# Earlier loads, a split cast and new step times in an attention and token-mixing kernel on one core

**Chip, cores, metric.** One core of one Trainium2 chip. The metric is device time of one execution in microseconds (us). TensorE is called PE here, VectorE DVE, ScalarE ACT, GpSimd Pool and SyncE SP, as in the profile. A profile's span is about 1.7 us shorter than the run's time.

## The reference, cut to what matters

```python
# q, k, v: (8, 8, 576, 64); p: (8, 8, 32, 64)
def sm_attn(qq, kk, vv):
    s = scale * np.matmul(qq, kk.transpose(0, 1, 3, 2))
    a = np.exp(s - np.max(s, axis=-1, keepdims=True))
    return np.matmul(a / (a.sum(-1, keepdims=True) + 1e-09), vv)
p_packed = sm_attn(p, k, v)                 # 32 packed tokens per head
attn     = sm_attn(q, p_packed, p_packed)   # (8, 8, 576, 64)
# heads side by side: x is (8, 576, 512)
W_tok = scale * np.einsum('bsd,btd->bst', x @ w_q, x @ w_k)
out   = np.maximum(np.einsum('bst,btd->bsd', W_tok, x), 0) @ w_out
```

## The kernel before: the parts concerned

All work of a batch is cut into some twenty kinds of steps. Each has a time within the batch; step time plus batch times period is sorted, and the steps are issued in that order. The times only set each engine's order. Where the data of its next step are missing an engine stands, with the steps behind it: in the trace of the kernel before PE was idle for 1.85 us at `pr` until the cast of p was done.

```python
TIMES = ((16.10, {"lk": (-18.66,), "lv": (-6.60,), "lq": (-5.91,), "vc": (0.67,),
                  "kt": (0.00, 2.23, 0.41), "sa": (3.00, 5.24, 2.46), "pv": (6.73,),
                  ...                                          # cut
                  "pr": (2.76,)}),
         (16.09, {"mx": ..., "oa": ..., "ob": ...}))           # cut
todo = sorted((t + b * period, b, name, c)
              for period, times in TIMES for name, ts in times.items()
              for c, t in enumerate(ts) for b in range(B))
for _, b, name, c in todo:
    steps[name](b, c)
```

`lk`, `lv` and `lq` load k, q (cast to bf16 on the way) and v (float32) from Pool's queue. `vc` casts v. `kt` and `sa` transpose k and make the packed tokens' exponentials; `pv` multiplies these with v in 144 small matmuls, each with its own weight load. `qt`, `sc`, `sm`, `at` do the second attention, `pq`, `wk`, `wq`, `g`, `y`, `mx` the mixing, `oa` and `ob` the two halves of an output block.

```python
def pr(b, _):                      # batches 1, 3, 5: casts and transposes p of b+1 and b+2
    if b % 2 == 1 and b + 1 < B:
        p_transposes((b + 1) // 2)     # DVE cast of p_sb, 8 PE transposes, two copies

def sa(b, c):
    ...                                # cut: 24 matmuls, one exponential
    if b == 0 and len([n for n in st[0] if n[0] == "e1"]) == NC3:   # behind the third one
        for i, w in enumerate((moe_w_q, moe_w_k)):
            nc.scalar.dma_start(w_first[:, :, i * Dl:(i + 1) * Dl], ...)
        nc.scalar.dma_start(p_sb[:, 1:], p_v[:, 1:])

def vc(b, _):
    ...                                # cut: batch 0 comes in three pieces
    nc.gpsimd.tensor_copy(to[:, :, :, 0:Dh], v_in[b])

def pq(b, _):
    if b == 0:
        for i in range(2):             # i = 0 on ACT, i = 1 on DVE
            copy(i, wqk[:, :, i * Dl:(i + 1) * Dl], w_first[:, :, i * Dl:(i + 1) * Dl])
    ...
```

The softmax here doesn't subtract the row's maximum and nothing guards it: scores larger than these inputs give would overflow.

## Time and profile before

| | before |
|---|---|
| median time (3 runs) | 163.94 us |
| span of the profile, granted PE clock | 161.7 us, 0.926 |
| busy: PE, DVE, ACT, Pool | 77, 54, 49, 44% |
| start, up to `pv` of batch 1 | 37.3 us |
| six batches, `pv` of 1 to `pv` of 7 | 94.1 us |
| end | 30.3 us |

The prediction shows how these parts are read. The six batches in one line, from the view of stretches (start:end, length, busy time of PE, its weight loads, DVE, ACT and Pool, then granted PE clock, DMA share and GB/s):

```profile
37.27:131.40 94.13, 76.83 (x2102) 57.57 (x2120) 58.89 (x135) 50.89 (x117) 47.15 (x49) 0.96 0.78 202
```

In these traces the clock is 0.5 or 1 at any moment, so a mean of 0.96 means half clock for some 8% of the stretch. The cut at 131.40 lies 0.4 us ahead of the first matmul of that `pv`; cut at the matmul, the six batches take 94.5 us and the end 29.9.

### The profile page before, as it was taken

The numbers are of one execution on the slowest core, as the hardware profiler recorded it, in microseconds if no ns is written. First come the engines' busy times: TensorE is split into PE (matmuls) and PEld (weight loads), VectorE is DVE, ScalarE is ACT, GpSimd is POOL, SyncE is SP. The second block draws the span as 40 slices with busy tenths as digits, with TensorE's granted clock in tenths as the row PEclk, the third lists the DMA queues.
The fourth block names the chain that finished last, engine by engine and source line by source line (L and its number), as shares of the span: only waits on it lengthen the run. The fifth ranks groups of instructions, "written<-read, shape, count | busy, mean of one in ns | idle before, by whom it ended". The sixth has DMA issues, their size and how long they took to land.

```text
span 161.7 us, 6522 instructions
## 1 busy us (share of the span) xinstructions
PE 124.6 (77%) x2877; PEld 86.3 (53%) x2904; DVE 87.5 (54%) x197; ACT 79.1 (49%) x172; POOL 71.1 (44%) x84
## 2 busy tenths in 40 slices
PE   4588289469497995699935986999884989999950
PEld 1255166237375873477533863777464757755410
DVE  7642047623397788368720688467743875861300
ACT  3133004151176374557801574466832775878750
POOL 7960003673049654905960074907920690460000
PEclk9999759957999999999996898699999999999995
DMA  4999999008940599599989932499889440565584
GB/s 137 369 261 282 284 199 236 27 0 284 218 90 6 128 298 233 148 289 231 259 246 296 224 79 69 103 332 229 255 233 262 147 121 19 137 178 143 152 230 140
DMA packets 15532, 30.63 MB, mean 189 GB/s; under 512 B 2704, under 2 KB 5264, under 8 KB 15504
## 3 DMA queue, kind: packets, MB, share of 16 engines
q0 software_dynamic: 6512, 17.63, 46.2%
q1 hardware_dynamic: 7536, 11.93, 24.0%
q10 hardware_dynamic: 1456, 0.66, 1.9%
q8 instruction: 22, 0.36, 0.9%
q14 instruction: 6, 0.05, 0.1%
HBM read 30.15 MB, written 9.44 MB: 245 GB/s over the span
## 4 chain that ended last, share of the span: by engine, by line
PE 64%; DMA 11%; issue 10%; DVE 7%; ACT 5%; ACTq 1%; DVEq 0%
PE out_ps L415 16%; DMA p_sb<-in_p_dram 10%; PE T_ps L208 9%; PE pv_ps L255 7%; PE e_ps L303 5%; DVE p_nat L159 4%; PE warm_ps L192 4%; PE mix_ps L384 4%; PE e_ps L237 4%; PE aT_ps L324 4%; PE wk_ps L332 3%; PE wq_ps L343 2%; ACT o_sb L116 2%; PE g_ps L356 2%; DMA out_dram<-o_sb 1%
## 5 line engine op out<-in xcount | busy, mean ns | idle before, releaser
L415 PE MATMUL out_ps<-wout_w,relu 128*128 128x512 bf16 x109 | 33.3, 389 | 0.8 <-issue 0.8
L116 ACT ACTIVATE o_sb<-out_ps 128x512 f32<-128x512 f32 x36 | 21.2, 597 | 8.6 <-PE out_ps L415 6.4
L297 DVE COPY qT<-T_ps 128x768 bf16<-128x768 bf16 x24 | 13.4, 558 | 7.0 <-PE T_ps L208 5.8
L192 PE MATMUL warm_ps<-warm 128*128 128x512 bf16 x33 | 16.2, 536 | 1.2 <-DVE warm L172 1.2
L228 DVE COPY kT<-T_ps 128x768 bf16<-128x768 bf16 x24 | 12.7, 536 | 6.0 <-PE T_ps L208 5.7
L116 ACT ACTIVATE wk<-wk_ps 96x128 bf16<-96x128 f32 x16 | 4.3, 272 | 22.3 <-PE wk_ps L332 22.2
L303 PEld LDWEIGHTS <-qT 128*96 128x96 bf16 x192 | 11.9, 128 | 3.9 <-issue 2.5
L208 PE MATMUL T_ps<-ident,k_sb 128*128 128x128 bf16 x144 | 12.8, 231 | 1.3 <-DVE k_sb L114 0.7
L208 PEld LDWEIGHTS <-k_sb 128*128 128x128 bf16 x144 | 10.4, 104 | 5.7 <-issue 1.8
L208 PE MATMUL T_ps<-ident,q_sb 128*128 128x128 bf16 x144 | 13.0, 229 | 0.0
L326 DVE COPY aT<-aT_ps 128x384 bf16<-128x384 bf16 x24 | 8.4, 353 | 8.2 <-PE aT_ps L324 8.1
L415 PEld LDWEIGHTS <-relu 128*128 128x128 bf16 x128 | 10.6, 102 | 4.1 <-issue 0.4
L373 DVE TENSOR_SCALAR relu<-mix_ps 128x512 bf16<-128x512 f32 x16 | 10.5, 661 | 2.9 <-PE mix_ps L384 2.7
L259 DVE RECIPROCAL rec<-pv_ps 128x2 f32<-128x2 f32 x8 | 1.4, 171 | 19.5 <-PE pv_ps L255 19.5
L384 PE MATMUL mix_ps<-wqT,y 128*128 128x512 bf16 x31 | 11.0, 403 | 0.1
L208 PEld LDWEIGHTS <-q_sb 128*128 128x128 bf16 x144 | 9.8, 105 | 1.2 <-issue 1.0
L268 POOL TENSOR_TENSOR ppb<-pp,mask 128x256 bf16<-128x256 bf16 x16 | 10.4, 667 | 0.0
L375 ACT ACTIVATE relu<-mix_ps 128x512 bf16<-128x512 f32 x16 | 9.2, 611 | 0.5 <-PE mix_ps L384 0.5
L332 PEld LDWEIGHTS <-aT 128*96 128x96 bf16 x96 | 7.6, 131 | 3.4 <-issue 0.8
L237 PE MATMUL e_ps<-pT,kT 128*32 128x64 bf16 x576 | 8.5, 202 | 0.6 <-issue 0.5
L303 PE MATMUL e_ps<-ppT_106,qT 128*96 128x64 bf16 x96 | 6.7, 213 | 2.5 <-issue 2.4
L332 PE MATMUL wk_ps<-pqk,aT 128*96 128x64 bf16 x96 | 8.1, 210 | 0.6 <-issue 0.2
(311 smaller groups left out, 271.0 us busy)
## 6 DMA issues: line engine op xcount, KB each, us to landing
v_in<-in_v_dram POOLq DMA_DIRECT2D x7, 1152.0 KB, 6.6
q_sb<-in_q_dram POOLq DMA_DIRECT2D x8, 576.0 KB, 9.5
out_dram<-o_sb SPq DMA_DIRECT2D x24, 192.0 KB, 2.4
k_sb<-in_k_dram POOLq DMA_DIRECT2D x7, 576.0 KB, 12.2
out_dram<-o_sb SPq DMA_DIRECT2D x24, 128.0 KB, 2.8
out_dram<-o_sb SPq DMA_DIRECT2D x24, 64.0 KB, 2.6
k_first<-in_k_dram SPq DMA_DIRECT2D x3, 384.0 KB, 3.9
v_first<-in_v_dram SPq DMA_DIRECT2D x3, 384.0 KB, 6.2
```

The lines of the kernel that those rows point to most:

```text
L116: nc.scalar.activation(o, i, COPY)
L192: nc.tensor.matmul(ps, warm[:, 0:P], warm, start=True, stop=True)
L208: nc.tensor.transpose(ps[:, r, G, :], x_sb[:, G, sls[r]:sls[r] + 2, :].rearrange("a r d -> a (r d)"), ident)
L228: nc.vector.tensor_copy(kT, ps)
L237: nc.tensor.matmul(ps[m, r, G], kT[:, r, G, m], pT[:, b, G * NP + pos], start=True, stop=True)
L255: nc.tensor.matmul(ps[m, G, 0:Dh + 1], e1[m, r, G, par, :], v_sb[m, G, s, 0:Dh + 1], start=s == 0 and G == 0, stop=s == R - 1, skip_group_ ...
L297: nc.vector.tensor_copy(qT, ps.rearrange("a r G (pos s) -> a (G pos) r s", s=QP))
L303: nc.tensor.matmul(ps[:, :, h, :], qT[:, h].rearrange("a r s -> a (r s)"), st[b]["ppT"][:, h], start=True, stop=True)
L332: nc.tensor.matmul(ps[:, par, :], st[b]["aT"][:, G, c, par, :], st[b]["pqk"][:, G, Dl:], start=G == 0, stop=G == NG - 1)
L373: nc.vector.tensor_scalar_max(o, i, 0.0)
L384: nc.tensor.matmul(ps, yT[:, j * P:(j + 1) * P], wqT[:, 0:SM], start=True, stop=True)
L415: nc.tensor.matmul(ps, lhsT, wout_w[:, j, :], start=j == 0, stop=j == NJ - 1)
```

## The change

Its intent: loads early enough that none can be late, v's cast shared between Pool and DVE in thirds, and times from a new search with a shorter period.

```diff
-        (16.10, {
-            "lk": (-18.66,),
-            "lv": (-6.60,),
-            "lq": (-5.91,),
-            "vc": (0.67,),
-            "kt": (0.00, 2.23, 0.41),
-            "sa": (3.00, 5.24, 2.46),
-            "pv": (6.73,),
+        (13.00, {
+            "lk": (-21.58,),
+            "lv": (-17.17,),
+            "lq": (-16.52,),
+            "vc": (2.56, -0.25, 4.48),
+            "kt": (0.00, 1.08, 3.20),
+            "sa": (3.17, 4.37, 4.45),
+            "pv": (7.57,),
   (cut: the other steps' times)
-            "pr": (2.76,),
+            "pr": (-2.43,),
   (cut: mx, oa, ob)
-    dve_relu = (0, 1, 1, 0)
-    dve_wk = (0, 1, 0)
-    dve_out = (0, 0, 0, 0, 0)
-    dve_g, dve_y = 1, 0
+    dve_relu = (0, 0, 0, 1)
+    dve_wk = (1, 1, 0)
+    dve_out = (0, 0, 0, 0, 1)
+    dve_vc = (0, 0, 1)
+    dve_g, dve_y = 0, 0
-    def vc(b, _):
+    def vc(b, c):
+        sl = slice(c * KR, (c + 1) * KR)
+        o = v_bufs[b % NV][:, :, sl, 0:Dh]
         if b == 0:
   (cut)
+        elif dve_vc[c]:
+            nc.vector.tensor_copy(o, v_in[b][:, :, sl])
         else:
-            nc.gpsimd.tensor_copy(to[:, :, :, 0:Dh], v_in[b])
+            nc.gpsimd.tensor_copy(o, v_in[b][:, :, sl])
```

More of the change, by code (lines that the diff above doesn't have):

```diff
@@ L63 @@
     TIMES = (
-        (16.10, {
-            "lk": (-18.66,),
-            "lv": (-6.60,),
-            "lq": (-5.91,),
-            "vc": (0.67,),
-            "kt": (0.00, 2.23, 0.41),
-            "sa": (3.00, 5.24, 2.46),
-            "pv": (6.73,),
-            "pb": (19.95,),
-            "pt": (8.98,),
-            "pq": (21.08,),
-            "qt": (10.55, 13.14, 12.71),
-            "sc": (12.87, 15.04, 13.77),
-            "sm": (14.55, 19.55, 15.12),
-            "at": (22.27, 22.89, 21.67),
-            "wk": (24.66, 25.55, 23.04),
-            "wq": (29.65, 30.21),
-            "g": (28.60,),
-            "y": (30.56,),
-            "pr": (2.76,),
-        }),
-        (16.09, {
-            "mx": (38.10, 38.52, 36.27, 38.58, 45.80),
-            "oa": (56.28, 40.85, 48.55, 46.70, 50.18),
-            "ob": (57.42, 43.99, 52.01, 49.34, 52.86),
-        }),
-    )
-    dve_relu = (0, 1, 1, 0)
-    dve_wk = (0, 1, 0)
+        (13.00, {
[6 more added lines that the diff above has]
+            "pv": (7.57,),
+            "pb": (16.38,),
+            "pt": (8.90,),
+            "pq": (16.84,),
+            "qt": (9.51, 10.76, 7.84),
+            "sc": (10.92, 13.87, 10.45),
+            "sm": (12.13, 15.24, 11.86),
+            "at": (16.52, 18.39, 20.21),
+            "wk": (20.16, 21.01, 22.26),
+            "wq": (20.58, 25.73),
+            "g": (25.03,),
+            "y": (27.49,),
+            "pr": (-2.43,),
+        }),
+        (13.02, {
+            "mx": (30.92, 29.75, 29.33, 29.75, 31.56),
+            "oa": (44.18, 36.27, 40.19, 34.22, 40.47),
+            "ob": (45.18, 37.85, 41.19, 36.33, 41.68),
+        }),
+    )
+    dve_relu = (0, 0, 0, 1)
+    dve_wk = (1, 1, 0)
     dve_wq = (0, 0)
-    dve_out = (0, 0, 0, 0, 0)
-    dve_g, dve_y = 1, 0
+    dve_out = (0, 0, 0, 0, 1)
+    dve_vc = (0, 0, 1)
+    dve_a2 = (0, 0, 0)
+    dve_g, dve_y = 0, 0
     def pool(name, bufs, psum=False):
@@ L211, in transposes @@
         return ps
-    def vc(b, _):
-        to = v_bufs[b % NV]
+    def vc(b, c):
+        sl = slice(c * KR, (c + 1) * KR)
+        o = v_bufs[b % NV][:, :, sl, 0:Dh]
         if b == 0:
-            for c in range(NC3):
-                copy(c != 1, to[:, :, c * KR:(c + 1) * KR, 0:Dh], v_first[:, c])
+            copy(c != 1, o, v_first[:, c])
+        elif dve_vc[c]:
+            nc.vector.tensor_copy(o, v_in[b][:, :, sl])
         else:
-            nc.gpsimd.tensor_copy(to[:, :, :, 0:Dh], v_in[b])
+            nc.gpsimd.tensor_copy(o, v_in[b][:, :, sl])
     def kt(b, c):
@@ L314, in sm @@
         a2 = six.tile([CH, 2 * H, L], bf16, tag="a2", name="a2")
-        nc.gpsimd.tensor_tensor(a2, e2, rr.to_broadcast((CH, 2 * H, L)), op=MULT)
+        (nc.vector if dve_a2[c] else nc.gpsimd).tensor_tensor(
+            a2, e2, rr.to_broadcast((CH, 2 * H, L)), op=MULT)
         st[b]["a2", c] = a2.rearrange("a (x G pos) l -> a x G (pos l)", x=2, G=NG)
```

## The prediction

> **What bounds the kernel now.** I first read the page's busy shares: the TensorE (PE) is busy 77% of 161.7 us, no other engine above 54%, and the transfers of the three large queues fill 46.2, 24.0 and 1.9% of the 16 DMA engines. So no engine is full, and the next question is where PE stands idle. I cut the span at the start of each batch's `pv` (its probabilities times v) in the view of stretches; columns are start:end, length, then each engine's busy time, PE's granted clock, DMA share and GB/s.
>
> ```profile
> 0.00:37.27 37.27, 24.33 (x428) 14.72 (x433) 17.42 (x37) 10.04 (x17) 17.83 (x29) 0.84 0.79 197
> 50.98:65.72 14.74, 12.02 (x356) 9.08 (x358) 11.47 (x26) 8.32 (x21) 9.55 (x11) 1.00 0.79 199
> 80.44:102.20 21.76, 15.23 (x358) 10.75 (x360) 11.56 (x26) 9.67 (x22) 8.94 (x11) 0.87 0.68 176
> 102.20:116.10 13.90, 13.64 (x355) 9.98 (x357) 9.29 (x23) 9.09 (x21) 8.21 (x9) 0.95 0.95 248
> 131.40:161.70 30.30, 23.45 (x351) 13.99 (x352) 11.19 (x27) 18.14 (x39) 6.16 (x8) 0.94 0.50 140
> ```
>
> A good batch is PE-bound: 13.64 of 13.90 us busy. Six steady stretches, from `pv` of batch 1 to `pv` of batch 7, take 94.1 us; the start takes 37.3 and the end 30.3. What makes a batch slower is in the timeline of PE (start, length, instructions, idle before them and its cause):
>
> ```profile
> 62.64 0.41 PE L163 MATMUL pT_ps<-ident,p_nat 128*64 128x128 bf16 x8 [1.84 <-DVE p_nat L159]
> ...
> 68.28 0.38 PE L255 MATMUL pv_ps<-v_bf_85,e_1539 32*32 32x65 bf16 x25 [1.43 <-issue]
> ...
> 86.59 0.26 PE L324 MATMUL aT_ps<-perm,a_2071 96*128 96x96 bf16 x1 [3.54 <-issue]
> ```
>
> The idle called "issue" breaks groups in mid-row: 23 of 48 matmuls, idle, then 25. No data can be missing there. The page lists a queue of 22 packets that carries instructions:
>
> ```profile
> q8 instruction: 22, 0.36, 0.9%
> ```
>
> 0.36 MB in 22 packets is 16 KB a packet. I set the packets' times beside the count of PE instructions. Each long "issue" gap falls at a multiple of about 255 PE records (447, 1211, 1721, 2486, 2995, 3251, 4525, 4780, 5290), and the gap ends 1.2 to 1.5 us after such a packet lands. The packet for the next block starts 0.5 to 1 us after PE enters the present one when no load is in flight, but 2.4 to 7.5 us after when a burst of loads is. A block that PE uses up faster than that ends in a stall, and `pv` alone is 288 instructions in 1.2 us. Such stalls after 37 us sum to 12.0 us (2.08, 0.62, 1.43, 0.72, 3.54, 0.94, 2.15, 0.56). Missing loads cost nothing there: no steady-state wait is put down to k, q or v.
>
> The start hangs on one transfer, as the chain that ended last shows (start, length, what):
>
> ```profile
> 16.53 13.54 DMA p_sb<-in_p_dram
> 30.09 1.14 DVE p_nat L159
> ```
>
> [...] while k and wout were loading, the queue of w_first and p_sb got about one packet for each of theirs (178 against 142 in the 2 us after 24 us). [...] the trace has half-clock stretches of 3.4 and 6.8 us, after idle at 16 to 20, 29 to 34, 83 to 87 and 96 to 98 us.
>
> **The change, part by part.** The step times only set each engine's order, so I sorted them for both kernels. PE's work is the same: 5,800 instructions.
>
> *Loads.* On Pool they stay where they were, three in a row behind `pb`; what differs is the batch. Before, behind pb of batch b came v and q of b+1 and k of b+2; now all three are of b+3. As no wait for them was on the path, being earlier saves nothing by itself. Two effects remain. The last burst falls near `pv` of batch 5, not of 6, so one burst fewer can delay instruction blocks. And v and q of batch 2 join the queue in the first 12 us.
>
> *The start.* That last effect meets the transfer of p. It is issued at 16.53 as before (behind the first three exponentials) and must pass 256 more packets of v and 256 of q. At one packet for one, with packets of 218 and 194 ns beside its own 46 ns (records of those queues), these take (218+46)x256/16 = 4.2 and (194+46)x256/16 = 3.8 us. p had some 560 packets left when k of batch 2 was through, at about 26.5, so it lands at about 34.7, not 29.7. At the same time step `pr`, which needs it, moves ahead: from behind kt of batch 1 (2.76+16.10 = 18.86) to 10.57, ahead of the last q transposes of batch 0, two of its three scores, and all of kt and sa of batch 1. VectorE and PE run in order, so both stop there from about 24.5 to 35.5, and PE then starts at half clock. What is left before `pv` of batch 1 is 6.7 us at full clock (24.69 to 29.4 and 31.27 to 37.27 in the trace, less waits), so 9 to 11 with the slow clock: `pv` of batch 1 begins near 46, not 37.3. **Plus 8.7 us.**
>
> *Casts of v.* Pool loses 2.10 us per batch and gains two thirds of that, 1.40; VectorE gains one 128x768 cast, 0.55 (the same shape from k_first takes 0.546). Pool is 44% busy and VectorE 54%: off the path. With relu, wk, g and output copies reassigned, ScalarE takes about 0.3 us more per batch (one relu of 0.61, g's 0.29 and less of wk's and an output), VectorE nearly none. Three relus now follow each other on ScalarE with pqk and three exponentials ahead of `pv`, 4.1 us of work where PE has 3.3: a small wait, 1 us in all six batches.
>
> *Order of PE.* Counting instructions through the new order tells where the blocks of 255 end. Short blocks, by the durations of the groups: 1.9 us (batch 1), 1.8 (2), 2.6 (3), 1.15 (4), 1.25 (5), 3.0 (6), 2.7 (7). Against about 3 us of undisturbed refill, and 5 or more within a burst (which will begin near the end of `pv`), that makes about 1, 1.7, 1, 1.9, 2.5, 0.3, 0.3: 8.7 us, of which 8.4 before `pv` of batch 7, against 11.5 there now. **Minus 3.1.** The later casts of p find only one third of a v cast on Pool beside them, and stand behind a score group in PE's order: waits of about 1.0 each, not 1.84. **Minus 1.7.** With the 3.5 us hole gone its half-clock stretches go too: **minus 3.**
>
> *Sum.* Start 46.0. Steady: 94.1 - 3.1 - 1.7 - 3 + 1 for ScalarE + 1.3 for output work done earlier = 88.6. End: 30.3 - 1.3 for that work - 0.3 for the stall + 0.8 because three of the last four relus share ScalarE = 29.5. That is 164.1 in the profile's span, against 161.7: plus 1.5%, or 166.4 us of the median of 163.94. I take off 2.4 because the order came from a search and I priced its stalls from few cases: **164.0 us**.
>
> **Rivals.** (1) *The start stays as it was and the steady gains are bare.* It would hold if p's packets passed faster, or if work held up at the start were hidden later. For it: PE after `pr` has a compact backlog, and before, too, it did little between 16 and 37 us. Then 161.7 - 8 + 1 = 155 in span, about 157 us. (2) *Refill stalls grow.* The bursts now start with k, its packets 2,304 B, and come a little earlier in the batch; if block fetches inside `pv` wait 5 to 7 us as at 66.7 and 82.8, add 5: 169 us. (3) *ScalarE or VectorE becomes the bound.* Estimated busy 10.6 and 10.8 us in a batch of 13 to 14.5: against it. If it came, about 0.5 us per batch: 167. (4) *The loads are hidden anyway* and only noise is left: 164; it agrees with my number by another way.
>
> **Range and chances.** The three runs before spread from 161.62 to 165.97, 2.7%. The start is uncertain by 2.5 us, stalls by 3, the rest by 2; together 4.4, so about 6 us either way: 157.5 to 170. Faster by over 2% needs under 160.7: 0.29. Slower by over 2%, above 167.2: 0.24. Within: 0.47.
>
> **What would show it.** Right: the cast of p of batches 2 and 3 starts at 34 to 36 us, with 8 us or more of idle PE before it and `pv` of batch 1 after 43; the steady six batches take 86 to 91 us; "issue" gaps at multiples of 255 records, summing to 7 to 10 us; no wait for k, q or v. Wrong: p landing by 30 (then packets do not alternate as I count), or steady batches under 13.5 us, which would make the change clearly faster; or new waits of PE on ScalarE of over 0.5 us a batch.

## The result

The changed kernel takes **173.74 us** (median of 4, 173.0 to 175.63) against 163.07 (median of 4): the ratio of the fast runs is 1.067, 95% interval 1.053 to 1.082. It is clearly slower, outside the predicted range. The ratio is the mean time of one kernel's fast runs over that of the other's of the same rounds, so not quite the ratio of the medians quoted.

Here a run counts as slow when it is over 1.5% above its kernel's fastest. On this one core times spread without a gap, 158.9 to 169.0 for the kernel before in 55 runs. For many kernels too few runs are left as fast, so I give medians of all runs too, and say where the two disagree. The profile of the changed kernel is of a run of 175.63, slow by this rule, 1.5% above the fastest; a second one (e1, 173.57, also slow) has the same parts.

| part | before | predicted | after | e1, the same kernel |
|---|---|---|---|---|
| start | 37.3 | 46.0 | 49.8 | 50.2 |
| six batches | 94.5 | 88.6 | 95.0 | 92.7 |
| end | 29.9 | 29.5 | 29.1 | 28.8 |

The same parts in the view of stretches of the changed kernel:

```profile
0.00:49.79 49.79, 25.38 (x438) 15.58 (x442) 19.66 (x40) 10.05 (x17) 19.72 (x32) 0.77 0.74 186
49.79:144.77 94.98, 79.53 (x2118) 59.33 (x2138) 60.12 (x138) 54.02 (x124) 45.29 (x54) 0.92 0.71 183
144.77:173.90 29.13, 21.98 (x333) 12.95 (x336) 9.95 (x24) 16.56 (x36) 4.46 (x6) 0.94 0.50 137
```

In the start PE is busy as long as before, 25.4 us against 24.3, within 12.5 us more. The steady part has not become shorter, and its clock is lower, 0.92.

PE's timeline tells where it stood (start, length, instructions, idle before them and what ended it):

```profile
11.35 0.51 PE L210 MATMUL T_ps<-ident,k_sb 128*128 128x128 bf16 x6 [1.60 <-ACT k_sb L118]
...
36.21 0.64 PE L165 MATMUL pT_ps<-ident,p_nat 128*64 128x128 bf16 x8 [11.36 <-DVE p_nat L161]
...
45.82 0.29 PE L293 MATMUL pqk_ps<-wqk,ppT_106 64*32 64x128 bf16 x8 [2.93 <-DVE wqk L116]
...
56.47 0.51 PE L210 MATMUL T_ps<-ident,q_sb 128*128 128x128 bf16 x6 [3.34 <-issue]
...
101.91 0.40 PE L259 MATMUL pv_ps<-v_bf_86,e_2154 32*32 32x65 bf16 x14 [5.54 <-issue]
```

The second gap is the step `pr` waiting for p, the great loss of the start. Before, PE waited at the same step for 1.85 us:

```profile
31.27 0.41 PE L163 MATMUL pT_ps<-ident,p_nat 128*64 128x128 bf16 x8 [1.85 <-DVE p_nat L159]
```

The transfer of p in the changed kernel is in the chain that ended last (start, length, what), and the DMA issues give size and time to landing:

```profile
17.60 18.24 DMA p_sb<-in_p_dram
```

```profile
p_sb<-in_p_dram ACTq DMA_DIRECT2D x1, 384.0 KB, 18.2
```

p now takes 18.2 us instead of 13.5 to land and is awaited ahead of all of `kt` and `sa` of batch 1. The 5.54 us at 101.91 breaks a group of 48 matmuls: a refill of instructions, as the prediction reads such gaps. A packet of the queue `q8 instruction` runs from 99.61 to 100.58 us and PE goes on 1.33 us after it has landed, while a burst of loads is in flight (its packets run from 95.1 to 106.6 us). e1 has the same gap of 5.54 us at the same place.

### The profile page after: what moved, and what is told of

The parts are those of the page before. It is cut to its first block, busy times and chain, and to the rows that moved or that the text cites.

```text
span 173.9 us, 6543 instructions
## 1 busy us (share of the span) xinstructions
PE 126.9 (73%) x2879; PEld 87.9 (51%) x2904; DVE 89.7 (52%) x200; ACT 80.6 (46%) x176; POOL 69.5 (40%) x91
## 4 chain that ended last, share of the span: by engine, by line
PE 60%; DMA 14%; issue 10%; DVE 4%; ACT 3%; POOL 3%; SPq 1%; ACTq 1%
PE out_ps L420 15%; DMA p_sb<-in_p_dram 10%; PE T_ps L210 10%; PE pv_ps L259 6%; PE e_ps L307 5%; PE mix_ps L389 4%; DMA v_first<-in_v_dram 4%; PE warm_ps L194 3%; PE e_ps L241 3%; PE aT_ps L329 3%; PE wq_ps L348 3%; PE wk_ps L337 2%; PE g_ps L361 2%; DVE wqk L116 1%; PE ppT_ps L278 1%
## 5 line engine op out<-in xcount | busy, mean ns | idle before, releaser
L118 ACT ACTIVATE o_sb<-out_ps 128x512 f32<-128x512 f32 x32 | 18.8, 594 | 7.0 <-PE out_ps L420 5.6
L301 DVE COPY qT<-T_ps 128x768 bf16<-128x768 bf16 x24 | 13.4, 558 | 12.6 <-PE T_ps L210 12.5
L194 PE MATMUL warm_ps<-warm 128*128 128x512 bf16 x34 | 17.2, 549 | 1.2 <-DVE warm L174 1.2
L354 ACT ACTIVATE wqT<-wq_ps 128x288 bf16<-128x288 f32 x16 | 6.6, 414 | 22.7 <-PE wq_ps L348 22.7
L210 PE MATMUL T_ps<-ident,q_sb 128*128 128x128 bf16 x144 | 13.7, 238 | 3.5 <-issue 3.3
L232 DVE COPY kT<-T_ps 128x768 bf16<-128x768 bf16 x24 | 12.5, 532 | 7.0 <-PE T_ps L210 6.7
L210 PE MATMUL T_ps<-ident,k_sb 128*128 128x128 bf16 x144 | 13.6, 235 | 2.9 <-ACT k_sb L118 1.6
L420 PEld LDWEIGHTS <-relu 128*128 128x128 bf16 x128 | 11.1, 103 | 6.0 <-issue 0.9
L380 ACT ACTIVATE relu<-mix_ps 128x512 bf16<-128x512 f32 x24 | 13.7, 606 | 0.4
L210 PEld LDWEIGHTS <-q_sb 128*128 128x128 bf16 x144 | 10.6, 109 | 5.1 <-issue 4.4
L272 POOL TENSOR_TENSOR ppb<-pp,mask 128x256 bf16<-128x256 bf16 x16 | 12.6, 806 | 0.0
L165 PE MATMUL pT_ps<-ident,p_nat 128*64 128x128 bf16 x32 | 2.1, 270 | 14.1 <-DVE p_nat L161 14.1
L319 POOL TENSOR_TENSOR a_534<-e_490,rr 96x512 bf16<-96x512 f32 x1 | 1.0, 1039 | 27.4 <-DVE rr L317 27.4
L389 PE MATMUL mix_ps<-wqT,y 128*128 128x512 bf16 x32 | 10.4, 382 | 0.3 <-ACT y L118 0.3
L118 ACT ACTIVATE pT<-pT_ps 64x512 bf16<-64x512 bf16 x4 | 2.4, 592 | 17.1 <-DVE pT L116 17.1
## 6 DMA issues: line engine op xcount, KB each, us to landing
v_in<-in_v_dram POOLq DMA_DIRECT2D x7, 1152.0 KB, 10.2
```

The lines of the kernel that those rows point to most:

```text
L118: nc.scalar.activation(o, i, COPY)
L194: nc.tensor.matmul(ps, warm[:, 0:P], warm, start=True, stop=True)
L210: nc.tensor.transpose(ps[:, r, G, :], x_sb[:, G, sls[r]:sls[r] + 2, :].rearrange("a r d -> a (r d)"), ident)
L232: nc.vector.tensor_copy(kT, ps)
L272: nc.gpsimd.tensor_tensor(ppb[:, G], st[b]["pp"][:, G, 0:1, :].to_broadcast((P, NP, Dh)), mask, op=MULT)
L301: nc.vector.tensor_copy(qT, ps.rearrange("a r G (pos s) -> a (G pos) r s", s=QP))
```

## The experiments

Sixteen runs were made, of eleven new kernels; the others repeat one of these or the change. "Mean" is the ratio of the means of all runs, "fast" that of the fast runs (a dash where one alone was fast). The runs e1 to e4 share a chip, so do e5 to e8, e9 to e12 and e13 to e16. "Steady" is `pv` of batch 1 to `pv` of batch 7 in the run's profile, "issue" PE's idle time so named within it, summed from the timeline (0.15 us and more). Weighed by fast runs alone, at 2%, the record calls the change slower, and every experiment "unclear" or, with too few fast runs, nothing at all; so what the profiles show is firmer below than what the times show.

| run | median us (runs) | before | mean | fast | `pv` of 1 at | steady | issue |
|---|---|---|---|---|---|---|---|
| before | 163.07 (4) | | | | 37.3 | 94.5 | 12.7 |
| after | 173.74 (4) | 163.07 | | 1.067 | 49.8 | 95.0 | 14.1 |
| e1 the change again | 174.66 (4) | 162.66 | 1.058 | - | 50.2 | 92.7 | 13.8 |
| e2 the change, `pr` late | 160.10 (4) | 162.66 | 0.977 | - | 38.9 | 92.9 | 8.5 |
| e3 the change, old load lead | 170.71 (4) | 162.66 | 1.042 | 1.037 | 44.9 | 92.1 | 12.8 |
| e4 before, `pr` early | 164.59 (4) | 162.66 | 1.005 | 1.004 | 41.0 | 89.0 | 10.2 |
| e5 before, `pr` late | 161.38 (4) | 164.01 | 0.976 | - | 35.6 | 90.8 | 6.8 |
| e6 e2, no loads from batch 3 | 151.40 (4) | 164.01 | 0.920 | 0.923 | 39.8 | 82.4 | 2.7 |
| e7 e2, v cast whole | 166.00 (4) | 164.01 | 1.007 | 1.013 | 37.4 | 96.4 | 9.1 |
| e8 e2, loads a batch later | 163.95 (4) | 164.01 | 0.996 | 0.994 | 38.1 | 94.2 | 4.6 |
| e9 e2, `pv` in thirds | 160.28 (20) | 164.08 | 0.976 | 0.982 | 35.3 | 93.3 | 5.5 |
| e10 e9, weights cast on ACT | 158.86 (4) | 164.08 | 0.964 | - | 34.1 | 93.9 | 7.4 |
| e11 e10, v from SP's queue | 160.30 (20) | 164.08 | 0.977 | 0.981 | 36.8 | 90.5 | 5.2 |
| e12 e2 again | 161.26 (20) | 164.08 | 0.985 | 0.995 | 37.0 | 93.6 | 9.0 |
| e13 e10, weights loaded first | 156.66 (6) | 164.87 | 0.951 | 0.944 | 32.3 | 94.7 | 5.5 |
| e14 e10 again | 156.47 (6) | 164.87 | 0.952 | 0.956 | 33.2 | 91.3 | 6.6 |
| e15 e7 again | 165.66 (22) | 164.87 | 1.006 | 0.983 | 39.9 | 97.3 | 11.2 |
| e16 e2 again | 162.40 (6) | 164.87 | 0.989 | 0.986 | 37.8 | 93.7 | 9.0 |

All but e6 give the right result. In e9 to e11, e13 and e14 the first third of `pv` stands earlier in the order, so their `pv` of 1 at is not to be compared with the others' to within 1 or 2 us.

**The start: where `pr` stands.** Theory A: the change lost its time to `pr`, at which DVE and PE stop until p has landed. Rival: the start only waits elsewhere. e1 is the changed kernel as it is, to be the measure on this chip.

> The changed kernel itself once more, for a profile in the fast state and a ratio of the same rounds. All theories: ratio to before 1.06 to 1.08; cast of p of batches 2 and 3 starts near 35 us after 10 to 12 us of idle PE; idle called issue of 12 to 16 us after the start.

It did as expected by its median (174.66 to 162.66); one of its four runs, the only fast one, took 168.01, which is 1.036 of the fast runs of before. So the size of the loss is known to some 3% only.

e2 moves one step and nothing else:

```diff
-            "pr": (-2.43,),
+            "pr": (8.00,),
```

> The changed kernel with one step moved: the cast and transposes of p for the batches after next go from 10.57 to 21.0 (behind pv of batch 1 in every engine's order; first needed by batch 2). Theory A (PE and VectorE stand still at this step until p lands, and nothing makes up for it): the 11 us of idle PE shrink to a wait for the weights' transfer of 0 to 4 us, pv of batch 1 begins at 39 to 42 us, time falls by 8 to 11 us to 162 to 166. Rival B (the time is lost in steady batches or to refills of instructions, the start only waits elsewhere): time falls by under 4 us.

14.6 us less by the medians, more than expected; 10.4 us less between the one fast run of each (157.65 and 168.01), as expected. By mean and median it is faster than the kernel before. PE's timeline of e2:

```profile
33.84 0.40 PE L293 MATMUL pqk_ps<-wqk,ppT 64*32 64x128 bf16 x8 [2.90 <-DVE wqk L116]
42.14 0.41 PE L165 MATMUL pT_ps<-ident,p_nat 128*64 128x128 bf16 x8 [0.85 <-DVE p_nat L161]
```

The 11.36 us at `pr` have become 0.85, while p landed no sooner (its last packet starts at 36.2 us in the trace, 36.0 in e1). The next wait in line, 2.90 us for the weights, is as long as in the change. `pv` of batch 1 begins 11.3 us earlier than in e1. Theory A holds, and the step's place alone makes up more than the whole loss.

e4 asks the same from the other side, with the kernel before:

```diff
-            "pr": (2.76,),
+            "pr": (-3.01,),
```

> The kernel before with one step moved, the other way: the cast of p for the later batches at the place that the change gives it (from 18.86 to 13.09 of 16.1 a batch). Theory A: VectorE and PE stop at it from about 24 to 30, pv of batch 1 moves from 37.3 to 42 to 45, time plus 4 to 7 us: 167 to 171. Rival: the work behind it is hidden by the later waits, within 2 us of before.

```profile
30.96 0.64 PE L163 MATMUL pT_ps<-ident,p_nat 128*64 128x128 bf16 x8 [7.93 <-DVE p_nat L159]
```

The wait is there, 7.93 us, and `pv` of batch 1 comes 3.7 us later than in the profile before, at 41.0 instead of 42 to 45. It moves by less than the wait because the waits before of 1.85 us for p and 1.92 us for the weights are taken up in it (0.81 us is left at the weights). But the time rose only by 1.9 us in the median, 0.4% in the fast runs: a miss for theory A, and the rival's number ("within 2 us of before") came true. Its profiled run had a steady part of 89.0 us, 5.5 us less than before, so the profile can't exclude that some of the start was made up later. With steady parts of one kernel varying by 2 us between profiles (95.0 and 92.7 for the change), 3.7 us of start are hard to see in four runs; the reverse test leaves theory A open for the kernel before.

e5 moves `pr` of the kernel before the other way, to 10.60.

> The kernel before with the cast of p for the later batches moved later too (from 18.86 to 26.7 of 16.1 a batch, behind the second batch's pv). Theory A: its own waits of PE for p and for the cast at 29 to 33 us go, pv of batch 1 begins 1 to 3 us earlier than 37.3, time 159 to 162; then the step times of the change, freed of this step, are worth little more than this. Rival: the wait is taken over whole by the cast of the weights behind it; no change within 1 us.

161.38 against 164.01, ratio of the means 0.976 (its one fast run: 158.19), and `pv` of batch 1 begins at 35.6, 1.7 us earlier, as theory A had it. The kernel before with this one step moved is as fast as the changed kernel with it moved (0.977, 0.985 and 0.989 in e2, e12 and e16). So all else in the change, new order, splits and earlier loads together, is worth nothing that these runs can show.

**The start: loads ahead of p.** e3 gives the changed kernel's loads the lead that they had before, counted in batches:

```diff
-            "lk": (-21.58,),
-            "lv": (-17.17,),
-            "lq": (-16.52,),
+            "lk": (-15.07,),
+            "lv": (-5.33,),
+            "lq": (-4.77,),
```

> The changed kernel with the loads at the same lead in batches as before (k 1.16, v 0.41, q 0.37 of a batch ahead). Theory: p no longer queues behind v and q of batch 2, lands near 30 instead of 35.8, so 4 to 6 us less: 167 to 170. Rival (the lead of the loads is not what delays p): p lands at 34 to 36 and the time stays at 172 to 175.

```profile
31.34 0.64 PE L165 MATMUL pT_ps<-ident,p_nat 128*64 128x128 bf16 x8 [4.91 <-DVE p_nat L161]
```

p's last packet starts at 30.6 us instead of 36.0, the wait is 4.91 us instead of 11.1 in e1, and `pv` of batch 1 begins 5.3 us earlier: v and q of batch 2 in the queue delay p by about the 5 us that the prediction gave them. The median falls by 4.0 us, at the edge of what was expected; but the two fast runs of e3 (167.86 and 168.33) are no faster than the one of e1 (168.01), so a gain in the whole time is not shown.

Are the early loads needed? e8 takes e2 and shifts all three by one batch (each time plus 13).

> e2 with all loads one batch later (k, v and q of batch b+2 behind pb of batch b, and only batch 1's at the start). Theory (the weights and p queue behind the loads of batch 2): the weights land by 26 and p by 28 us, the wait of 2.9 us for the weights' cast goes, time 2 to 4 us under e2: 156 to 158. Rival (loads needed this early): waits for k, v or q of over 1 us a batch and more time than e2.

The last packet of p starts at 27.0, as the theory said. But the wait for the weights stayed at 2.90, and new waits came:

```profile
107.67 0.51 PE L210 MATMUL T_ps<-ident,k_sb 128*128 128x128 bf16 x6 [1.00 <-DMA k_sb<-in_k_dram]
124.61 0.82 PE L210 MATMUL T_ps<-ident,k_sb 128*128 128x128 bf16 x6 [3.46 <-DMA k_sb<-in_k_dram]
```

The rival was right: with 8.58 of 13 us as its lead k is late, and e8 is no faster than before. The lead of 1.16 batches that k had before is enough: in e3, with that lead, no wait for k, q or v is listed behind those of batch 0. The change's longer lead (half a batch for k, nine tenths for v and q) delays p at the start, and has no return that shows.

Why the 2.90 us did not go, though the weights had landed at 26.6, shows in the timelines of DVE and Pool in e8, beside that of DVE in the kernel before:

```profile
30.38 2.50 DVE L116 CAST wqk<-w_first 64x512 bf16<-64x512 f32 x1
31.94 1.94 POOL L272 TENSOR_TENSOR ppb<-pp,mask 128x256 bf16<-128x256 bf16 x2
```

```profile
33.01 0.35 DVE L114 CAST wqk<-w_first 64x512 bf16<-64x512 f32 x1
```

The same cast took 0.35 us while Pool was all but idle (its next instruction starts at 33.23), and 2.50 us beside Pool's casts and products from 27.37 to 33.84 us. Its end follows Pool, and not its own start: it came 0.28 us after the first of the two `ppb` products ended (32.60), and so it did in nine other profiles (the change, e1 to e3, e6, e7, e12, e15, e16), by 0.28 to 0.29 us, though the cast had begun 1.06 to 3.03 us earlier. So in these runs the "wait for the weights" was a wait for Pool's chain, and an earlier transfer could not shorten it.

**The steady part: refills of instructions.** Theory C: they wait behind the bursts of loads. Rival D: they are slow by themselves, or the stores delay them. e6 is e2 with a wrong result: no loads from batch 3 on.

```diff
     def load_k(b):
+        if b > 2:
+            k_in[b] = k_in[2]
+            return
   (cut: the same for q and v)
```

> e2 without any load of k, q, v from batch 3 on (wrong result on purpose: batches 3 to 7 use batch 2's inputs). Theory C (blocks of instructions wait behind the bursts of loads): after the start the issue gaps of PE sum to 3 to 6 us, not 8 to 14, none over 2 us from batch 2's pv on, the six steady batches take 82 to 87 us, not 93, and the run 148 to 154. Rival D (refills are slow by themselves, or the stores delay them): gaps stay at 8 us or more and the time falls by under 3 us.

The steady part of e6, then that of e16, which is e2 with its loads:

```profile
39.80:122.20 82.40, 76.86 (x2139) 56.34 (x2142) 59.97 (x140) 54.45 (x125) 36.87 (x42) 0.99 0.27 71
```

```profile
37.80:131.50 93.70, 80.66 (x2135) 58.25 (x2134) 60.14 (x140) 54.45 (x125) 45.38 (x54) 0.94 0.71 184
```

The same work takes 11.3 us less. The issue gaps fall from 9.0 to 2.7 us, all other idle from 4.0 to 2.8, and the clock rises from 0.94 to 0.99: half clock for 10.6 us, against 1.4, which costs up to 4.6 (an estimate: half of the difference). Theory C holds, with gaps even under the 3 to 6 us expected, in so far as the loads as a whole are the cause: without them, the rest of the work at this order runs at 13.7 us a batch. e6 also frees Pool of issuing them (54 instructions against 42), but PE's idle time for other causes than issue fell by 1.2 us only. The clock, too, fell behind the long stalls: in e16 half clock follows the gaps of 2.36 and 3.53 us, and none follows those of 0.83 to 1.30. The stores have a part too: ahead of the 3.54 us hole of the kernel before, the refill's packet started 1.8 us after its block was entered, while stores filled 71% of the DMA engines and loads 20% (packets that start from 81.5 to 83.25 us), and then took 2.00 us beside the loads, about double the 0.98 us that is the median of the 22 such packets of that trace.

e9 attacks the stall from the other end: `pv` in three steps of 96 instructions with other work between.

```diff
-            "pv": (7.57,),
+            "pv": (5.30, 6.30, 7.57),
   (cut: oa of block 3 from 34.22 to 33.25, its ob from 36.33 to 34.30)
-    def pv(b, _):
+    def pv(b, c):
+        if c == 0:
+            st[b]["pv"] = psum(w_pool, [P, NG, VW], fp32, "pv_ps")
+        ps = st[b]["pv"]
-        for s in range(R):
+        for s in range(c * KR, (c + 1) * KR):
   (cut: the rest of `pv` runs with the third step alone)
```

> e2 with pv in three steps of 96 instructions each, the first and second with an output half, a transposition and a mix between them, the third behind an earlier output half; no instruction is added. Theory C [...]: blocks around pv last longer, the issue gaps after the start sum to 4 to 8 us instead of 9 to 14, time 2 to 5 us under e2's 160. Rival: gaps only move to other places, within 1 us of e2.

Beside e12, the same chip and 20 runs each: 160.28 against 161.26, 0.982 against 0.995 by the fast runs. The issue gaps fell from 9.0 to 5.5 us, into the expected band; the time fell by 1 to 1.5 us, less than expected. The intervals of the two ratios overlap (0.976 to 0.989; 0.984 to 1.006), so the gain is likely, not shown. A new wait of 0.69 us for v stands ahead of the earlier `pv` of batch 2.

> e2 once more, as the measure of the other runs of this call on the same chip: 0.97 to 1.00 of before.

e11 breaks up the burst: v of batches 4 to 7 is issued by SP between two stores.

> e10 with v of batches 4 to 7 loaded from the SyncE queue between two stores, some 3 us of PE's order after k and q, so that a burst is k and q alone. Theory C: shorter bursts beside pv, refill delays there fall from 4 us, 1 to 3 us less. Rival: the bytes are the same and the delays only spread: no change within 1 us, or waits for v.

160.3 against 158.86 of e10 and 160.28 of e9: the rival. In its profile the issue gaps are shorter than in e10 (5.2 against 7.4 us) and so is the steady part, while the start is 2.7 us longer; in 20 runs nothing is gained.

**Casts of v.** e7 is e2 with v cast whole on Pool.

> e2 with v cast whole on Pool again, in one instruction. Theory (off the path): within 1.5 us of e2's 160. Rival (the split saves a wait ahead of pv): 2 us or more slower, with waits of PE for the v cast in pv.

166.00 against 160.10 of e2: the rival's number, but on another chip, so it was run again beside e2:

> e7 (v cast whole on Pool) beside e2 on one chip, since they were on different chips. If the split of v's cast itself saves time: 2 to 5 us slower than e16. If e7 was slow by its chip: within 1.5 us of e16.

> e2 for the third time, as the measure of e15 on the same chip: 0.97 to 1.00 of before.

PE's timeline of e15:

```profile
34.83 0.40 PE L290 MATMUL pqk_ps<-wqk,ppT 64*32 64x128 bf16 x8 [3.95 <-DVE wqk L116]
...
56.55 1.51 PE L256 MATMUL pv_ps<-v_bf,e 32*32 32x65 bf16 x144 [1.17 <-POOL v_bf L220]
```

Both gaps are of the same length in e7's profile: at the weights' cast 1.05 us longer than in e2 and e16, where Pool's casts of v are short, and a wait of 1.17 for v in batch 2. Those 2.2 us are shown, and so is that the rival had the wait right. By the medians e15 is 3.3 us slower than e16, and by the means 2.7, but the fast runs of both are equal (0.983 and 0.986), so how much of it stays in the whole run is not settled.

**A better version.** e10 adds to e9 that both halves of the weights' cast run on ACT (`copy(0, ...)` for `copy(i, ...)`).

> e9 with both halves of the weights' cast on ScalarE. Theory (the cast on VectorE took 1.06 to 2.50 us beside Pool's work and held PE 2.9 us at pqk): wait at pqk of batch 0 shrinks by 0.5 to 1.5 us and pv of batch 1 begins that much earlier; the whole run changes by as little.

> e10 once more with more rounds, as the measure of e13: 0.96 to 0.98 of before.

e14 took 156.47 us against 164.87 of before, fast ratio 0.956 (0.943 to 0.970). The wait for the weights was 3.43 us in e10's profile, 1.57 in e14's; and on ACT the second half of the cast starts as soon as the weights land (31.07 and 30.79). What of the gain over e9 is this cast, I cannot tell from so few runs.

e13 also issues the weights' loads first of all on ACT's queue, and casts them behind the third exponential.

> e10 with the two loads of the weights issued first of all on ScalarE's queue (before: behind the third exponential, in the middle of the loads) and cast there behind the third exponential. Theory: PE's wait of 3.4 us at pqk of batch 0 goes, and p has fewer packets ahead of it; the first k pieces land up to 1 us later; pv of batch 1 begins 2 us earlier than in e10; time 1 to 3 us under e10. Rival: a new wait in the start takes its place, within 1 us of e10.

The wait at `pqk` is gone from the timeline and p's last packet starts at 25.6, but 156.66 us is e14's time: the first `kt` pieces waited 2.15 us instead of 1.42 for k, and the steady part of its profile was 3.4 us longer. The rival, within the spread of these runs. Both versions take about 5% less than the kernel before, and by the ratios to it some 10% less than the change.

## Why the prediction was wrong

Its direction of the start and the way that p is delayed were right. Three terms of its sum were mis-sized, and a fourth had no ground. The sum of 164.1 us came out 173.9 in the profile: 3.8 us of the difference lie in the start, 6.4 in the six batches and -0.4 in the end. Its own rival (2), "Refill stalls grow", because the bursts "come a little earlier in the batch", is what came in the steady part.

1. **"Order of PE ... Minus 3.1."** The refill stalls of the steady part were to be 8.4 us, against 11.5 before; counted in the same way, without gaps under 0.5 us, they were 13.7 (with the small gaps 14.1, against 12.7). The step that failed is the cost of a refill in batches 1 and 4: it was priced near "about 3 us of undisturbed refill", because the burst "will begin near the end of `pv`". There PE took 6.2 and 6.8 us from entering one block to going on in the next (2.9 and 3.05 in the estimate), and the stalls were 3.34 us (estimated 1) and 5.54 (estimated 1.9). In the other four batches the stalls sum to 4.8 us, against 5.5 estimated, each within 1 us. I had counted Pool's chain behind `sc` as longer than PE's path to the end of `pv`. In fact the first load of the burst was issued 3.2 us ahead of the start of `pv` in batch 1 and 1.2 ahead in batch 4, and 1.4, 0.3 and 0.3 us behind it in batches 2, 3 and 5; its packets follow 1.5 to 1.8 us later. That the earlier burst is the whole cause of these two stalls is not shown: in batch 4 of the kernel before 4.3 us of stalls came with a burst issued 0.7 us behind the start of `pv`, and in e16 batch 4 had 1.0 us with a burst issued 0.6 ahead. No run moves the burst alone. Pool's and PE's lines of batch 4:

```profile
93.58 0.77 POOL L128 DMA_DIRECT2D k_sb<-in_k_dram  x1
```

```profile
94.81 0.88 PE L259 MATMUL pv_ps<-v_bf_86,e_2058 32*32 32x65 bf16 x48
```

   Moreover, my range of refill delays ("2.4 to 7.5 us") was read too widely: where a block's first instruction had itself waited, I counted from the block before it. Counted from the end of the stall, a refill started 2.4 to 4.6 us after PE entered the block within a burst, in the kernel before.

2. **"With the 3.5 us hole gone its half-clock stretches go too: minus 3."** The hole did not go, it became 5.5 us. Half clock in the steady part rose from 8.2 us to 14.8 (10.5 in e1): up to 3.3 us more (half of the rise, an estimate) instead of 3 less. Of the two half-clock stretches meant, of 3.4 us each, one stands behind the hole, but the other, from 100.1 us, behind a wait of 1.84 us for the cast of p. What sets it is not shown: behind the same wait of 1.84 us at 62.64, and behind the gap of 2.15 at 124.5, the same trace has none.

3. **"Plus 8.7 us"** for the start was 12.5. The cast of p began at 35.86, inside the predicted 34 to 36, and PE was idle 11.36 us. Two waits were left out: 1.60 us (4.05 in e1) at the second piece of k, whose cast on ACT stands behind one of v that waits for its load (before, that piece came last), and 2.93 us at `pq` for the weights' cast on DVE, 2.28 us long, again until 0.28 us after Pool's product. I had taken the trace "less waits", and such a wait stood there before too, 1.92 us.

4. **"I take off 2.4"** because the order came from a search. The sum without it was 166.4; the search's order earned nothing (e5 beside e2).

Right were: no wait for k, q or v behind those of batch 0 in the changed kernel; issue gaps at block ends; waits of PE on ACT in the steady part under 0.3 us; the end, 29.1 against 29.5. Better than predicted were the later casts of p: no wait of 0.2 us or more, not 1.0 each, at 0.29 us a cast. That the end came so near is not evidence for its three terms, which no run tests singly. "Off the path" for v's cast was off by some 2 us early on (e7, e15), and VectorE's third of the cast, put at 0.55 us, took 0.75 to 1.82 us in batches 2 to 7, beside Pool's work.

Some readings of the working were wrong without moving its sum. Behind `pb` of batch b, the kernel before issues v and q of b+2 and k of b+3, not of b+1 and b+2. The gaps are multiples of 255 PE records apart, but do not stand at such multiples (447 is the first). In the 2 us after 24 us, k and wout together have 174 packets against the 178 quoted; 142 are k's alone.

## What to carry to other kernels

Here one early step that waited for a late transfer held up all the work behind it on its engine (11.36 us of idle PE at `pr`, 0.85 with the step moved, e2): before moving a step, ask when its data land, and when its result is first needed (here 1.4 batches later). Loads further ahead than their first use required were not free: with them in the queue p, which the start hangs on, took 18.2 us to land, and 11.8 in e3 without. And where PE stalls in mid-group without a data wait, look at the queue that carries instructions and count instructions per microsecond (in the kernel before PE went on 1.2 to 1.5 us after such a packet had landed, at stalls that are multiples of 255 PE records apart); whether it pays to spread the dense groups is not settled here (e9: likely, 1 to 1.5 us). Last, the wait put down to DVE's cast of the weights was here a wait for Pool (the cast ended 0.28 to 0.29 us after a Pool product in ten profiles): compare when a wait ends over several runs, not only how long it is.

## What the traces show of refills, casts and queues

- Refills of instructions, for a PE with some 2,900 matmuls and as many weight loads: 12.7 us of issue gaps in 94.5 us before, 14.1 of 95.0 after, and 2.7 of 82.4 without loads (e6). In the kernel before, counted in blocks of 255 PE records, the packet for the next block starts 0.5 to 1.1 us after PE enters a block with no load in flight and 2.4 to 4.6 us after it within a burst; the 22 packets take 0.9 to 2.0 us each; and at a stall PE goes on 1.2 to 1.5 us after the packet has landed.
- Casts of DVE beside Pool's work: the 64x512 cast from float32 took 0.35 us with Pool all but idle (the kernel before), 1.06 (e2), 2.28 (the change) and 2.50 us (e8) beside Pool's casts and products; a 128x256 cast took 0.28 to 0.29 us in e1 and e4, and 1.12 us in the kernel before beside Pool's cast of v. The first 128x256 cast, begun at 2.94 us in the kernel before and at 3.00 in the change, took 2.80 and 2.74 us, in both until 0.15 us after a Pool fill of 2.65 us. In e8 the 64x512 cast stood through three Pool instructions in a row, and ended 0.28 us after the third.
- Queues: in the 2 us after 24 us of the kernel before, 178 packets of the weights and p started beside 174 of k and wout. The small transfers have many small packets (640 KB, 1,408 of 256 and 1,024 bytes, with medians of 31 and 46 ns), and the loads beside them packets of 2,304 and 4,608 bytes (192 and 178 ns): p, the last part of the small ones, took 13.5 us to land before, and 18.2 with v and q of batch 2 in the queue as well.
